# Attention, MoE and soft MoE on one core: w_out turned for its product with phi, converted again after the attention

## The chip, the cores and the metric

The kernel runs on one core of one Trainium2 chip. The metric is the device time of one execution in microseconds (us), the lower the better; times are medians over runs. The engines are TensorE (PE, with its weight loads as PEld), VectorE (DVE), ScalarE (ACT), GpSimd (POOL) and SyncE (SP), which issues every DMA of this kernel.

## What is computed

Three layers, one after the other. Attention with rotary embedding over 4 batches of 8 heads, 576 positions, 64 wide; a feed-forward layer; a soft mixture of 8 experts with 4 slots each. The inputs of the last two, w_in and w_out among them, are float64 arrays; q, k and v are float32.

```python
# attention, then
h = x @ w_in                                   # (2304, 512) @ (512, 2048)
g = np.maximum(h, 0.0) + alpha * np.minimum(h, 0.0)
x = g @ w_out                                  # (2304, 2048) @ (2048, 512)
# soft mixture of experts
logits = x @ phi                               # (2304, 512) @ (512, 32)
d = softmax(logits over tokens); slot_input = d.T @ x
slot_out = relu(slot_input @ w1[e]) @ w2[e]    # 4 slots for each of 8 experts
return softmax(logits over slots) @ slot_out
```

## The kernel before

**The algebra.** x = g @ w_out is never formed. The logits are g @ (w_out @ phi), and the slots' inputs are (d.T @ g) @ w_out. So w_out is wanted twice: early, for the product wph = w_out @ phi (2048 by 32), and late, for the product px = (d.T @ g) @ w_out, after all tokens have been gone through.

**The stages.** The attention runs over 16 pairs of heads (4 batches, 4 pairs each). For a pair PE makes scores (st), DVE takes their maximum (mm), ACT the exponential (e), POOL scales it by the inverse sum (e<-e,mm). The block is then turned: in batch 0 by PE (pt), in batches 1 to 3 by DVE in 32-wide blocks (tb), which go through DRAM (sc) and come back turned (ET). PE then multiplies with v (pv); there are three pv for a pair, 48 in all. Beside the attention, and after it, the feed-forward layer goes over 9 blocks of 256 tokens (the last one gathers the rows beyond 512 of the four batches), each in 16 chunks of 128 hidden columns. A chunk is 12 matmuls (ph), rl on ACT, g on DVE; for two chunks PE turns g (pt) and ACT copies it (gt); for four chunks PE makes the logits (lg) with wph as weights, in four column groups side by side. Each block ends with pu, the sum d.T @ g. After the ninth block come px with w_out, the experts' two layers (ph of L1088, po) and the output (pf).

**The weights before.** prep_w (L593) brings w_in and then w_out in eight pieces each, 1 MB of float64 in a slot "raw", and DVE converts them to float32 by three integer steps (L628, L630, L632). A piece of w_out lands as 256 rows in a buffer of which there is one (wf, the tile w32; the trace calls it w). From there it goes two ways. A DMA stores it to wo_dram, a copy in DRAM in float32 (L659). And wphi (L675), twice for a piece, makes 128 rows of wph: PE turns four 128x128 blocks (wtp, L683), ACT copies them (wt, L687), PE multiplies the four with phi, w_out's blocks as weights and phi's 32 columns moving (wphp, L692), and DVE scales the result into wph (L695). After the attention the copy is read back (wo, L959) into a pool of 26 slots of 512 KB (x), which it shares with the experts' weights (xw, L995).

**What sets the order.** A planner (class Plan) takes every operation with a cost, a due time, what it depends on and the slots that it takes, and writes each engine's instructions in one fixed order. Each engine then runs its own list in order and waits by semaphores where something is not ready. The pool pm has three PSUM buffers, shared by ph, pt, pv, pu, wtp, wphp and others; PE can start a ph only when an earlier one has been read by rl and g.

## Time and profile before

| | |
|---|---|
| median of 3 runs | 688.85 us (685.62 to 688.97) |
| the profiled execution | 688.74 us, of which the span from first to last instruction is 686.9 us |
| mean granted TensorE clock | 0.958 of full speed |
| busy share of the span | PE 92%, PEld 66%, DVE 63%, ACT 48%, POOL 41% |
| moved by DMA | 160.76 MB, mean 234 GB/s |

All times in the rows are counted from the span's start; what lies outside the span, 1.8 us, is the same for any change inside. A busy share over the whole span mixes the stages: about 0 to 140 us (the first batch, with the weights' conversion), to 522 us (batches 1 to 3, with the first blocks of the feed-forward layer beside them), to 618 us (the rest of that layer alone), and the end (px, the experts, the output). So each stage is read by itself: the table of stretches tells how full each engine was, with the granted clock, the share of time in which the DMA engines were busy and what they moved; the timeline shows instructions with the idle time ahead of them in brackets and what ended it; the chain of waits follows the last instruction back through what released each step. Matmuls overlap in PE's pipeline, so a matmul's own duration is longer than its share of PE's time; that is read from one start to the next.

### The profile page before, as it was taken

The numbers are of one execution on the slowest core, as the hardware profiler recorded it, in microseconds if no ns is written. First come the engines' busy times: TensorE is split into PE (matmuls) and PEld (weight loads), VectorE is DVE, ScalarE is ACT, GpSimd is POOL, SyncE is SP. The second block draws the span as 40 slices with busy tenths as digits, with TensorE's granted clock in tenths as the row PEclk, the third lists the DMA queues.
The fourth block names the chain that finished last, engine by engine and source line by source line (L and its number), as shares of the span: only waits on it lengthen the run. The fifth ranks groups of instructions, "written<-read, shape, count | busy, mean of one in ns | idle before, by whom it ended". The sixth has DMA issues, their size and how long they took to land.

```text
span 686.9 us, 13841 instructions
## 1 busy us (share of the span) xinstructions
PE 629.2 (92%) x5168; PEld 453.5 (66%) x5168; DVE 429.7 (63%) x937; ACT 328.7 (48%) x816; POOL 283.4 (41%) x283
## 2 busy tenths in 40 slices
PE   2889979989999999998999999999999999988974
PEld 1555555667978678777777867777686878763442
DVE  5777798776968776686667868575743232334332
ACT  3536446444656566555465655564443433330121
POOL 0797998566237286376365554431210000000000
PEclk9878999968999999999999999999999999999996
DMA  9944275765499999989988989894465950457998
GB/s 302 369 157 148 76 265 177 216 210 181 141 282 253 301 269 290 271 239 267 280 230 253 272 262 269 215 249 137 135 160 211 401 217 9 154 177 274 368 391 284
DMA packets 78306, 160.76 MB, mean 234 GB/s; under 512 B 9888, under 2 KB 39072, under 8 KB 78240
## 3 DMA queue, kind: packets, MB, share of 16 engines
q1 hardware_dynamic: 78240, 159.88, 75.4%
q8 instruction: 41, 0.67, 0.4%
q14 instruction: 25, 0.20, 0.1%
HBM read 104.54 MB, written 34.08 MB: 202 GB/s over the span
## 4 chain that ended last, share of the span: by engine, by line
PE 56%; DMA 23%; DVE 7%; POOL 5%; SPq 4%; issue 2%; ACT 2%; DVEq 0%; ACTq 0%; POOLq 0%
PE ph L720 19%; PE pv L554 10%; DMA ET<-sc 8%; DMA sc<-tb 5%; DMA xw<-in_moe_w_dram 4%; PE st L412 4%; PE st L399 3%; PE pt L739 3%; PE pt L475 2%; PE lg L750 2%; PE pu L844 2%; SPq L508 2%; DMA ks<-xn 2%; PE wphp L692 2%; POOL e L454 2%
## 5 line engine op out<-in xcount | busy, mean ns | idle before, releaser
L454 POOL TENSOR_SCALAR e<-e,mm 128x576 f32<-128x576 f32 x144 | 120.0, 844 | 164.4 <-DVE mm L430 119.5
L720 PE MATMUL ph<-xt,w 128*128 128x256 f16 x1536 | 185.6, 273 | 0.1
L720 PEld LDWEIGHTS <-w 128*128 128x128 f16 x1728 | 163.9, 98 | 31.8 <-issue 11.0
L422 ACT ACTIVATE e<-st,mm 128x576 f32<-128x576 f32 x144 | 106.3, 739 | 43.4 <-DVE mm L417 34.9
L417 DVE TENSOR_REDUCE mm<-st 128x1 f32<-128x576 f32 x144 | 106.1, 744 | 23.3 <-PE st L412 12.6
L733 DVE SCALAR_TENSOR_TENSOR g<-rl,oma,ph 128x256 f32<-128x256 f32 x144 | 68.1, 473 | 82.0 <-ACT rl L728 81.2
L728 ACT ACTIVATE rl<-ph 128x256 f32<-128x256 f32 x144 | 55.2, 383 | 102.1 <-PE ph L720 101.1
L321 POOL TENSOR_TENSOR xn<-xn,tabs 128x576 f32<-128x576 f32 x60 | 88.8, 1491 | 36.7 <-issue 8.2
L554 PE MATMUL pv<-ET,vt 128*64 128x256 f32 x512 | 66.1, 400 | 10.2 <-DMA ET<-sc 8.9
L462 DVE STREAM_TRANSPOSE tb<-e 128x512 f32<-128x512 f32 x96 | 66.6, 700 | 11.9 <-DMA sc<-tb 6.0
L412 PE MATMUL st<-ks,qs 128*128 128x288 f32 x384 | 71.0, 313 | 0.2
L399 PE MATMUL st<-ks 64*128 64x288 f32 (+1 forms) x168 | 46.3, 497 | 16.6 <-DVE ks L329 11.2
L412 PEld LDWEIGHTS st<-ks,qs 128*128 128x128 f32 x384 | 54.5, 191 | 6.1 <-issue 3.3
L554 PEld LDWEIGHTS pv<-ET,vt 128*64 128x64 f32 x512 | 37.3, 141 | 30.8 <-issue 5.0
L744 ACT ACTIVATE gt<-pt 128x512 f32<-128x512 f32 x72 | 43.0, 598 | 12.4 <-PE pt L739 10.2
L399 PEld LDWEIGHTS st<-ks 64*128 64x128 f32 (+1 forms) x168 | 25.8, 209 | 31.1 <-DVE ks L329 11.2
L739 PE MATMUL pt<-idf,g 128*128 128x128 f32 x288 | 43.9, 275 | 0.4 <-DVE g L733 0.4
L564 ACT ACTIVATE xt<-pv,vb 128x256 f16<-128x256 f32 x32 | 15.1, 473 | 53.9 <-PE pv L554 53.9
L324 POOL TENSOR_TENSOR xn<-xn 128x576 f32<-128x576 f32 x24 | 36.0, 1502 | 1.1
L739 PEld LDWEIGHTS pt<-idf,g 128*128 128x128 f32 x288 | 33.4, 141 | 4.2 <-issue 2.4
L475 PE MATMUL pt<-idf,e 128*128 128x128 f32 x192 | 33.7, 310 | 2.6 <-POOL e L454 2.0
L475 PEld LDWEIGHTS pt<-idf,e 128*128 128x128 f32 x192 | 26.0, 163 | 14.2 <-issue 6.1
(155 smaller groups left out, 833.3 us busy)
## 6 DMA issues: line engine op xcount, KB each, us to landing
sc<-tb SPq DMA_DIRECT2D x48, 512.0 KB, 5.8
ET<-sc SPq DMA_DIRECT2D x96, 256.0 KB, 6.0
xw<-in_moe_w_dram SPq DMA_DIRECT2D x42, 512.0 KB, 9.4
ks<-xn SPq DMA_DIRECT2D x96, 144.0 KB, 4.5
xn<-in_k_dram SPq DMA_DIRECT2D x16, 576.0 KB, 5.8
xn<-in_q_dram SPq DMA_DIRECT2D x16, 576.0 KB, 6.6
wraw<-in_moe_w_in_dram SPq DMA_DIRECT2D x8, 1024.0 KB, 7.7
wraw<-in_moe_w_out_dram SPq DMA_DIRECT2D x8, 1024.0 KB, 5.6
```

Of the source, the lines that this page charges most:

```text
L321: eng.tensor_tensor(e["x"][:, w], e["x"][:, w], tabs[:, (0 if z == "q" else 2) + w], ALU.mult)
L399: nc.tensor.matmul(st[to, j, at:at + w], x, k[rows, z:z + w], start=True, stop=True)
L412: nc.tensor.matmul(st[:, j, 0:288], r["q"][:, 768 * h + 128 * s:768 * h + 128 * s + 128].bitcast(F32R), r["k"][:, a, h, ks].bitcast(F32R), ...
L417: nc.vector.tensor_reduce(c["mm"][:, h:h + 1], c["st", h][:, :, 0:288], axis=AX.XY, op=ALU.max, negate=True)
L422: nc.scalar.activation(c["e"][:, h].rearrange("p (a n) -> p a n", a=2), c["st", h][:, :, 0:288], AF.Exp, bias=c["mm"][:, h:h + 1], accum_o ...
L454: nc.gpsimd.tensor_scalar(c["e"][:, h], c["e"][:, h], c["mm"][:, 6 + h:7 + h], 1.0, ALU.mult, ALU.mult)
L462: nc.vector.transpose(out=c["tb"][:, :, h].rearrange("p (q m) j -> p q m j", q=4), in_=c["e"][:, h, 64 * h:64 * h + 512].rearrange("p (m q ...
L475: nc.tensor.transpose(c["pt", h][:, i], c["e"][:, h, 64 * h + 128 * i:64 * h + 128 * i + 128], idf)
L554: nc.tensor.matmul(pv[r], v[k, 4 * h + i if i < 4 else 8], x, start=(i == 0), stop=(i == 4))
L720: nc.tensor.matmul(ph, wi[j][:, wp, kc, 128 * fo:128 * fo + 128], xt[:, xp, kc, :], start=(n == 0), stop=(n == 3 * KC - 1),)
L733: nc.vector.scalar_tensor_tensor(blk["g", j][:, fo, :], c["r"], oma[:, f:f + 1], c["ph"], ALU.mult, ALU.add)
L739: nc.tensor.transpose(c["pt"][:, t, i, :], blk["g", j][:, fo - 1 + i, 128 * t:128 * t + 128], idf)
```

## The change

The host hands the kernel w_out a second time, turned (w_out_t, 512 by 2048). The early path loads pieces of w_out_t instead of w_out, 256 of its columns at a time, and converts them as before. The product with phi now has phi as weights: each of the four 128-row parts of phi is loaded into its own group of 32 columns (tile_position), all four multiply side by side into one PSUM tile (wpp), each giving a partial sum over its part of w_out's columns. ACT copies that (wt), and two matmuls with the columns' selector sel4 as moving operand turn it and add up the four groups (wphp). One wphi serves 256 rows of wph, so there are 8 in place of 16. The store to wo_dram is gone. When the attention ends, sixteen pieces of w_out in its natural form, 512 KB of float64 each, are loaded into slots of the pool x, and DVE converts each of them by the same three integer steps into the eight wo tiles, from which px reads as before. These loads are due ahead of the experts' weights.

```diff
-            if which == 0:
-                src = w_in[:, PF * j:PF * j + PF].rearrange("(c p) f -> p c f", p=128)
-            else:
-                src = w_out[PF * j:PF * j + PF, :].rearrange("(c p) f -> p c f", p=128)
-            nc.sync.dma_start(raw[:].rearrange("p (c f) t -> p c (f t)", c=src.shape[1]), src.bitcast(I32))
+            src = (w_in, w_out_t)[which][:, PF * j:PF * j + PF].rearrange("(c p) f -> p c f", p=128)
+            nc.sync.dma_start(raw[:].rearrange("p (c f) t -> p c (f t)", c=KC), src.bitcast(I32))
...
-            wo_saved.append(op(DMA, 1500, due, lambda: nc.sync.dma_start(wo_dram[:, 2 * j:2 * j + 2, :], c["wo"]), [o], uses=[s_w]))
-            for i in range(2):
-                wphi(2 * j + i, i, c, o, s_w, due + WS)
+            wphi(j, c, o, s_w, due + WS)
...
-        def turn():
-            c["p"] = ps_m.tile([128, KC, 128], F32, tag="pm", name="wtp")
+        def parts():
+            c["p"] = ps_m.tile([128, PF], F32, tag="pm", name="wpp")
             for i in range(KC):
-                nc.tensor.transpose(c["p"][:, i, :], w["wo"][:, z, 128 * i:128 * i + 128], idf)
+                nc.tensor.matmul(c["p"][32 * i:32 * i + 32, :], phs[:, i, :], w["wo"][:, i, :], start=True, stop=True, tile_position=(0, 32 * i))
...
         def mults():
-            c["q"] = ps_m.tile([128, NS], F32, tag="pm", name="wphp")
-            for i in range(KC):
-                nc.tensor.matmul(c["q"], c["t"][:, i, :], phs[:, i, :], start=(i == 0), stop=(i == KC - 1))
+            c["q"] = ps_m.tile([128, 2, NS], F32, tag="pm", name="wphp")
+            for z in range(2):
+                nc.tensor.matmul(c["q"][:, z], c["t"][:, 128 * z:128 * z + 128], sel4[:, 0], start=True, stop=True)
...
-        def reload(j=j):
-            wo[j] = xp["p"].tile([128, 2, 512], F32, tag="x", name="wo")
-            nc.sync.dma_start(wo[j], wo_dram[:, 2 * j:2 * j + 2, :])
-
-        wo_op[j] = op(DMA, 1456, 1000 + WO_AT, reload, [att_done] + wo_saved, takes=[s_wo[j]], uses=[s_wo[j]])
+        def load():
+            c["raw"] = xp["p"].tile([128, 512, 2], I32, tag="x", name="wor")
+            nc.sync.dma_start(c["raw"], w_out[128 * f:128 * f + 128, :].bitcast(I32).rearrange("p (d t) -> p d t", t=2))
+
+        def conv(step):
+            lo, hi = c["raw"][:, :, 0], c["raw"][:, :, 1]
+            if step == 0 and not z:
+                wo[j] = xp["p"].tile([128, 2, 512], F32, tag="x", name="wo")
+            x = wo[j][:, z].bitcast(I32)
+            if step == 0:
+                nc.vector.tensor_scalar(x, hi, 3, 0x3FFFFFFF, ALU.logical_shift_left, ALU.bitwise_and)
+            elif step == 1:
+                nc.vector.scalar_tensor_tensor(x, lo, 29, x, ALU.logical_shift_right, ALU.bitwise_or)
+            else:
+                nc.vector.scalar_tensor_tensor(x, hi, -0x40000000, x, ALU.bitwise_and, ALU.bitwise_or)
+
+        d = 990 + 0.1 * f
+        o = order_ops["wo"] = op(DMA, 1456, d, load, [att_done, order_ops.get("wo")], takes=[s_raw], uses=[s_raw])
+        o = op(DVE, 450, d, lambda: conv(0), [o, wo_op.get(j)], takes=[] if z else [s_wo[j]], uses=u)
+        o = op(DVE, 750, d, lambda: conv(1), [o], uses=u)
+        wo_op[j] = op(DVE, 700, d, lambda: conv(2), [o], uses=u)
```

The planner then orders all engines anew. Three places show it. On PE, in batch 0 (st are scores, pt and pc turn the exponentials e, pv multiplies with v, w32 is a converted piece of w_out), the kernel before has:

```order
L683 MATMUL wtp_1048<-idf_94,w32_988 128x128 x4
L399 MATMUL st_1054<-ks_705 128x288 x2
L692 MATMUL wphp_1070<-phs_104,wt_1058 128x32 x4
L475 MATMUL pt_1079<-idf_94,e_986 128x128 x4
L683 MATMUL wtp_1090<-idf_94,w32_988 128x128 x4
L475 MATMUL pt_1098<-idf_94,e_986 128x128 x4
L399 MATMUL st_1105<-ks_705 128x288 x2
L518 MATMUL pc_1109<-idf_94,e_986 128x128
L399 MATMUL st_1114<-ks_705 128x288 x2
L692 MATMUL wphp_1119<-phs_104,wt_1103 128x32 x4
L475 MATMUL pt_1131<-idf_94,e_1065 128x128 x4
```

and with the change:

```order
L676 MATMUL wpp_1060<-w32_984,phs_104 32x256 x4
L475 MATMUL pt_1066<-idf_94,e_961 128x128 x4
L518 MATMUL pc_1080<-idf_94,e_961 128x128
L685 MATMUL wphp_1084<-sel4_106,wt_1076 128x32 x2
L399 MATMUL st_1089<-ks_704 128x288 x2
L475 MATMUL pt_1097<-idf_94,e_1015 128x128 x4
L554 MATMUL pv_1103<-ET_986,vt_150 64x256 x8
L554 MATMUL pv_1103<-ec_1024,vt_150 64x256 x2
```

A piece of w_out took two sets of wtp and wphp, 16 matmuls, and takes one wpp and one wphp, 6 matmuls; the scores, turns and pv around it stay, in a somewhat other order. The last of the 8 wpp stands ahead of the first ph, where before four of the 16 sets stood among the ph.

On DVE, behind the end of the attention (dn, sacc, ssum and lp belong to a block's end, g to its chunks), the kernel before has:

```order
L836 TENSOR_SCALAR dn_6357<-pd_6339,vb_107 128x64
L733 SCALAR_TENSOR_TENSOR g_6327<-rl_6370,oma_113,ph_6344 128x256
L853 SCALAR_TENSOR_TENSOR sacc_117<-sacc_117,sts_115,pu_6361 128x512
L859 SCALAR_TENSOR_TENSOR ssum_114<-ssum_114,sts_115 128x1
L733 SCALAR_TENSOR_TENSOR g_6327<-rl_6397,oma_113,ph_6375 128x256
L733 SCALAR_TENSOR_TENSOR g_6434<-rl_6430,oma_113,ph_6399 128x256
L733 SCALAR_TENSOR_TENSOR g_6434<-rl_6441,oma_113,ph_6417 128x256
```

and with the change, in a stretch of chunks of that stage:

```order
L967 TENSOR_SCALAR wo_6399<-wor_6282 128x512
L969 SCALAR_TENSOR_TENSOR wo_6301<-wor_6256,wo_6301 128x512
L728 SCALAR_TENSOR_TENSOR g_6404<-rl_6401,oma_112,ph_6368 128x256
L971 SCALAR_TENSOR_TENSOR wo_6301<-wor_6256,wo_6301 128x512
L728 SCALAR_TENSOR_TENSOR g_6404<-rl_6413,oma_112,ph_6386 128x256
L969 SCALAR_TENSOR_TENSOR wo_6399<-wor_6282,wo_6399 128x512
L967 TENSOR_SCALAR wo_6451<-wor_6322 128x512
L971 SCALAR_TENSOR_TENSOR wo_6399<-wor_6282,wo_6399 128x512
L728 SCALAR_TENSOR_TENSOR g_6404<-rl_6453,oma_112,ph_6421 128x256
L967 TENSOR_SCALAR wo_6399<-wor_6303 128x512
L728 SCALAR_TENSOR_TENSOR g_6404<-rl_6464,oma_112,ph_6438 128x256
```

Between two g, which followed each other directly, now stand one to five steps of the conversion (wor is a piece of w_out as loaded, wo the converted tile).

On SP, the queue of DMA issues, at the end of the attention (sc and ET are its shuttle through DRAM), the kernel before has:

```order
L508 DMA ET<-sc 32x8x256 x4
L995 DMA xw<-in_moe_w_dram 128x1024 x18
L959 DMA wo<-wo_dram 128x1024 x2
L995 DMA xw<-in_moe_w_dram 128x1024
L959 DMA wo<-wo_dram 128x1024 x6
L995 DMA xw<-in_moe_w_dram 128x1024
L995 DMA xw<-in_moe_w_dram 128x2x1024 x7
```

and with the change:

```order
L499 DMA sc<-tb 128x1024 x2
L508 DMA ET<-sc 32x8x256 x4
L959 DMA wor<-in_moe_w_out_dram 128x1024 x16
L1014 DMA xw<-in_moe_w_dram 128x1024 x20
L1014 DMA xw<-in_moe_w_dram 128x2x1024 x7
```

The sixteen loads of w_out stand ahead of the experts' weights, where the eight reloads stood behind eighteen of them.

## Rows read from the trace of the kernel before

**Rows 1.** Stretches: us, busy us (instructions) of PE, PEld, DVE, ACT, POOL; clock, DMA share, GB/s
```profile
90.00:140.00 50.00, 44.79 (x283) 29.65 (x283) 41.71 (x68) 27.74 (x65) 37.83 (x33) 0.93 0.70 225
140.00:195.00 55.00, 53.52 (x387) 43.34 (x386) 43.84 (x87) 27.76 (x70) 27.65 (x27) 0.84 0.60 181
195.00:250.00 55.00, 52.03 (x465) 40.16 (x464) 39.94 (x89) 31.71 (x86) 28.66 (x30) 1.00 0.99 282
...
540.00:580.00 40.00, 39.91 (x372) 31.39 (x371) 13.07 (x30) 15.56 (x36) 0.00 (x0) 1.00 0.48 186
```

**Rows 2.** Chain of waits, 85 to 200 us: shares by line; pieces with start and us
```profile
by line: PE pv L554 13.1%; PE st L399 11.9%; PE wphp L692 10.7%; PE pt L475 6.5%; DMA ET<-sc 5.3%; PE ph L720 4.7%; PE wtp L683 4.3%; SPq L352 4.1%; issue 3.9%; DVE wx L630 3.8%; PE st L412 3.8%; DVE wx L632 3.0%; POOL e L454 2.9%; DVE xn L
...
143.06 0.61 ACT wt L687
...
166.27 1.08 PE wphp L692 x8
...
198.45 1.70 PE pv L554 x13
```

**Rows 3.** Groups by form: count, busy us, mean ns, then idle us before and releaser
```profile
L750 PE MATMUL lg<-g,wph 128*32 128x256 f32 x288 | 23.0, 391 | 0.0
...
L692 PE MATMUL wphp<-phs,wt 128*128 128x32 f32 x128 | 18.4, 290 | 2.2 <-ACT wt L687 2.2
```

**Rows 4.** Timeline of PE around two sets of lg: start, us, instruction, idle before
```profile
187.41 0.64 PE L750 MATMUL lg<-g,wph 128*32 128x256 f32 x8
187.98 1.08 PE L692 MATMUL wphp<-phs,wt 128*128 128x32 f32 x8
...
548.89 2.52 PEld L720 LDWEIGHTS <-w 128*128 128x128 f16 x24 [0.41 <-issue]
548.90 2.79 PE L720 MATMUL ph<-xt,w 128*128 128x256 f16 x24
```

**Rows 5.** Chain of waits, the pu that end two successive blocks
```profile
561.54 1.85 PE pu L844 x16
...
591.98 1.85 PE pu L844 x16
```

**Rows 6.** Timeline of DVE, conversion of the first piece of w_in, POOL idle
```profile
14.24 0.68 DVE L628 TENSOR_SCALAR w<-wraw 128x1024 int32<-128x1024 int32 x1
...
15.51 1.22 DVE L630 SCALAR_TENSOR_TENSOR w<-wraw,w 128x1024 int32<-128x1024 int32 x1
```

**Rows 7.** Timeline of DVE and PE after the attention, two pairs of chunks
```profile
550.84 0.48 DVE L733 SCALAR_TENSOR_TENSOR g<-rl,oma,ph 128x256 f32<-128x256 f32 x1 [1.94 <-ACT rl L728]
...
551.96 2.78 PE L720 MATMUL ph<-xt,w 128*128 128x256 f16 x24
...
552.14 0.48 DVE L733 SCALAR_TENSOR_TENSOR g<-rl,oma,ph 128x256 f32<-128x256 f32 x1 [0.83 <-ACT rl L728]
...
553.89 0.48 DVE L733 SCALAR_TENSOR_TENSOR g<-rl,oma,ph 128x256 f32<-128x256 f32 x1 [1.27 <-ACT rl L728]
```

**Rows 8.** DMA issues, us to landing: 521:523, 526:530 (xw), whole span (wraw)
```profile
xw<-in_moe_w_dram SPq DMA_DIRECT2D x3, 512.0 KB, 5.4
...
xw<-in_moe_w_dram SPq DMA_DIRECT2D x5, 512.0 KB, 9.6
...
wraw<-in_moe_w_in_dram SPq DMA_DIRECT2D x8, 1024.0 KB, 7.7
wraw<-in_moe_w_out_dram SPq DMA_DIRECT2D x8, 1024.0 KB, 5.6
```

**Rows 9.** The page: moved by DMA in 40 equal slices of 17.2 us
```profile
GB/s 302 369 157 148 76 265 177 216 210 181 141 282 253 301 269 290 271 239 267 280 230 253 272 262 269 215 249 137 135 160 211 401 217 9 154 177 274 368 391 284
```

**Rows 10.** Stretches of 1 us, PE alone: busy us, granted clock, DMA share, GB/s
```profile
143.00:144.00 1.00, 0.29 (x3) 1.00 1.03 360
144.00:145.00 1.00, 1.00 (x8) 0.50 0.48 105
...
161.00:162.00 1.00, 1.00 (x9) 0.96 1.05 400
```

More of the change, by code (lines that the diff above doesn't have):

```diff
@@ L162, in attn_moe_softmoe @@
 @with_exitstack
-def attn_moe_softmoe(ctx, tc, qx, kx, vx, w_in, w_out, alpha, phi, w1, w2, tab, msks, out):
+def attn_moe_softmoe(ctx, tc, qx, kx, vx, w_in, w_out, alpha, phi, w1, w2, tab, msks, w_out_t, out):
     nc = tc.nc
@@ L581, in attn_moe_softmoe @@
     wi = {}
-    wo_dram = dram.tile([128, FC, DM], F32, name="wo_dram")
-    wo_saved = []
     w_ops = {}
@@ L601, in load @@
             raw = c["raw"] = wgt.tile([128, 1024, 2], I32, tag="w", name="wraw")
[L602 to L608 removed]
+            src = (w_in, w_out_t)[which][:, PF * j:PF * j + PF].rearrange("(c p) f -> p c f", p=128)
+            nc.sync.dma_start(raw[:].rearrange("p (c f) t -> p c (f t)", c=KC), src.bitcast(I32))
+        a_, f_ = ((2, 128), (1, 256))[which]
         def conv(step):
@@ L953, in attn_moe_softmoe, with late_w @@
     wo, s_wo, wo_op = {}, {}, {}
-    for j in range(NPC):
-        s_wo[j] = Slot("x")
-        def reload(j=j):
-            wo[j] = xp["p"].tile([128, 2, 512], F32, tag="x", name="wo")
-            nc.sync.dma_start(wo[j], wo_dram[:, 2 * j:2 * j + 2, :])
-        wo_op[j] = op(DMA, 1456, 1000 + WO_AT, reload, [att_done] + wo_saved, takes=[s_wo[j]], uses=[s_wo[j]])
+    def late_w(f):
+        c, j, z = {}, f // 2, f % 2
+        s_raw = Slot("x")
+        if not z:
+            s_wo[j] = Slot("x")
+        u = [s_raw, s_wo[j]]
+        def load():
[17 more added lines that the diff above has]
+        wo_op[j] = op(DVE, 700, d, lambda: conv(2), [o], uses=u)
+    for f in range(FC):
+        late_w(f)
     NX = NB - 4
@@ L1355 @@
     form = {"q": _keys, "k": _keys, "v": _values, "moe2_w2": _second}
-    data = [(name, form[name](_np, a) if name in form else a) for name, a in data] + _tables(_np)
+    turned = [("w_out_t", _np.ascontiguousarray(a.T)) for name, a in data if name == "moe_w_out"]
+    data = [(name, form[name](_np, a) if name in form else a) for name, a in data] + _tables(_np) + turned
     for name, a in data:
```

21 lines of the change are left out of this document (11 added, 10 removed).

## The prediction

> **What bounds the kernel now.** The first view is the table of stretches. From 140 us to the end of the attention TensorE (PE) is busy for all but some percent of the time, and from 540 to 580 us for 39.91 of 40 us [rows 1]; POOL and ACT are far from full there. In 195 to 250 us the DMA share is 0.99 as well, so the attention of batches 1 to 3 is bound by two things at once, PE and the shuttle of transposed blocks through DRAM; after the attention the DMA falls idle while PE stays full. The second view is the chain of waits from 85 to 200 us, the stretch of the work that the change replaces. Before about 108 us it runs through DVE and POOL, from there to 185 us almost only through PE: of its 115 us, 10.7% are wphp, 4.3% wtp [rows 2]. So a PE microsecond taken out there is worth up to one microsecond, unless DMA, DVE or the clock takes it back.
>
> **What goes.** On the chain stand 12.3 us of wphp and 4.9 us of wtp (the two shares of 115 us), and three waits of PE for the copy wt on ACT, about 0.7 us each (the copy's 0.61 us, and the hand-overs; PE's own idle time ahead of wphp is 2.2 us in all) [rows 2, 3]. That is 17.2 + 2.1 = 19.3 us. The rest of the 16 sets lies beside DVE and POOL work and counts for nothing.
>
> **What comes in its place.** Eight times four wpp matmuls, 32 columns of weights by 256 moving, f32, in four column groups. That is the shape of lg, whose eight records take 187.41 to 187.98 us, 0.57 us, until the next starts [rows 4]. Then two matmuls with the shape of wphp, half of a set of four, 0.5 us (sets at full clock take 1.08 us with their overlap) [rows 2]. 8 x 1.07 = 8.6 us, all put on the path. Bounds: 6.5 of the 8 on the path give 7 us; four groups one after another instead of side by side would be eight records of 0.39 us [rows 3], 3.1 us a set, 25 us in all and 29 with the second step. I take 8.6, since the row has the same shape and the same four groups. So PE is relieved of 10.7 us.
>
> A rule speaks against this: the Trainium skill, TensorEngine Tiling (Array Packing), Key Properties, says that changing the tiling mode drains TensorE. The trace agrees in so far as the weight load behind an lg stands idle for 0.41 us, at 548.89 us, with PE's matmul 0.01 us behind it [rows 4]; but the 0.57 us run from start to next start, so a drain is in them. Were 0.41 us a switch to come on top at 16 switches, 6.6 us of the relief would be gone, and the sum at the end would be 689.0.
>
> **Where the relief lands.** The order shows it. Ahead of the 13th pv (198.45 us before [rows 2]) PE had 8 ph chunks done and now has 12; ahead of the 48th and last, 96 before and 98 now. A chunk costs 1.9 us of PE: 16 of them and their dispatch take 591.98 - 561.54 = 30.4 us [rows 5]. So of 10.7 us, 7.6 go into four chunks done early, and 3.1 us make the 13th pv earlier. From there to the end of the attention two chunks fewer are left: 3.8 us if PE is the bound, nothing if the DMA is (0.99 [rows 1]); between the two I take the middle, 1.9. After the attention two chunks fewer remain, on a PE without gaps: 3.8 us. Sum 3.1 + 1.9 + 3.8 = 8.8 us.
>
> **The late conversion.** Sixteen times three DVE steps on 128x512, behind the attention's end. On 128x1024 with POOL idle a tensor_scalar took 0.68, a scalar_tensor_tensor 1.22 us [rows 6]; halved, 0.34 + 0.61 + 0.61 = 1.6 us each, 25 us in all. The order spreads the 48 steps over 23 chunks, about 44 us, in which DVE has 23 x 0.48 = 11 us of g; it ends up some 85% full. What hides them: the gaps ahead of g, 0.83 and 1.27 us by turns (longer when lg stands between) [rows 7]. The order puts one step in the short gaps, two or three in the long ones, so a g is late by 0.1 to 0.4 us. What that may cost: the next ph but one needs g's PSUM buffer; g at 550.84 us ends at 551.32 and that ph starts at 551.96, so some 0.6 us are spare [rows 7]. Most lateness vanishes there. The first step waits for its load: the first loads of this stretch land 5.4 us after issue, later ones 9.6 [rows 8], and behind that waiting step stand g and the sacc update, for which PE waits through its three PSUM buffers. Conversions then come every 2.75 us, loads every 1.3 us (512 KB at about 400 GB/s [rows 9]), so only the first can be late. I take 2.5 us; bounds 0 and, if every step were uncovered, 25 us.
>
> **Edits taken at nothing.** Eight stores to wo_dram and eight reloads go; nothing on PE waits for them. SP now issues 16 raw loads of 512 KB first, then the expert weights, which wait for conversions to free slots. That is 4.2 MB more; covered by the DMA's idle time from 567 to 618 us (9, 154, 177 GB/s where 391 are possible: 17.2 us x 833 = 14 MB [rows 9]); without this cover 4.2 MB would cost 10.7 us. The weights for ph at 630 us then have 50 us to spare, and the tail (weights in slots that wo frees) keeps its order. The turned w_out comes in 2 KB runs, as w_in does: 7.7 against 5.6 us to land [rows 8]; three raw slots hide it. ACT loses 16 copies of 0.6 us and gains 8 shorter ones; DVE loses eight small scalings. The wf buffer no longer waits for a store, so the eight conversions of w_out move earlier, into a stretch with DVE 83% busy [rows 1]; that is why the 13th pv is only 3.1 us earlier in my sum.
>
> **Sum.** 688.74 (profiled execution; the median of the runs shown is 688.85) - 8.8 + 2.5 = 682.4 us.
>
> **Rivals.** (1) All of the relief is won and more. PE ran at half clock from 144 to 161 us, after idle time at 143 us [rows 10]; the waits for wt are part of that idling (143.06 us, [rows 2]). Without them the stretch may stay at 2.4 GHz: 17.4 us at half speed, less the 5.5 us of wphp and wtp in it already counted, halved: 6 us. 688.74 - 10.7 - 6 + 2.5 = 674.5. Against it: less work leaves more gaps, not fewer.
> (2) DMA and DVE bind: the 13th pv comes no earlier, the shuttle takes as long; left are the 3.8 us behind the attention, 688.74 - 3.8 + 2.5 = 687.4. For it: DMA 0.99; against it: PE's few idle microseconds.
> (3) The late conversion surfaces: DVE's fixed order makes g late beyond its 0.6 us. At 0.3 us lost for each of 48 steps, 14.4 us: 694.3, slower. It decides from 8.8 / 48 = 0.18 us a step. For it: DVE 85% full; against: the order fits steps to gaps.
> (4) A second stretch at half clock: with PE thinner from 90 to 165 us, another 17.4 us at 1.2 GHz where PE is the bound costs 8.7: 688.74 - 8.8 + 2.5 + 8.7 = 691.1. The Trainium skill, TensorE: Matmul & The Clock Gate, Part 1, says that the clock is 1.2 GHz after idling and 2.4 after sustained work; the trace agrees with the fall behind the idle 143rd us. By that rule alone, thinning PE's work would give this fourth time.
> (5) The column groups run one after another: 29 instead of 8.6 us, 702.
>
> **Chances.** Forecast 0.47 (own range 679 to 685.5), rivals 0.16, 0.18, 0.10, 0.07, 0.02. The range 672 to 690 takes in (1) and (2) and most of the forecast, and leaves out (3), (5) and half of (4). A measurement tells about 0.5%, 3.4 us, from no change: faster 0.61 (forecast but for its edge, and 1), same 0.22 (2, the edge, a little of 4), slower 0.17.
>
> **What will show it.** Right: wpp sets of about 0.57 us; 12 ph chunks ahead of the 13th pv, and that pv near 195 us; the last pv near 517 us; PE still without gaps from there to the last pu; conversions done some 45 us after the attention; the tail from px on as long as now. Wrong: clock below 1.00 in other stretches than before, ph waiting for DVE's g after the attention, the 13th pv at 198 us or later, expert weights waited for at ph (L1107), or wpp records that do not overlap.

## The result, and the profile with the change

| | before | with the change |
|---|---|---|
| median | 687.09 us (682.01 to 690.38, 20 runs) | 694.91 us (688.71 to 698.22, 20 runs) |
| ratio, 95% interval | | 1.0121 [1.0096, 1.0145] |
| profiled execution, its span | 688.74 us, 686.9 us | 689.75 us, 687.6 us |

The change makes the kernel slower by 1.2%, some 8 us, where 6.3 us of gain were forecast. The profiled execution of before is one of its slower ones, that of the change one of its faster ones; so the two traces differ by less than the medians, and where a few us matter the runs below decide, not these two traces. Ratios leave disturbed runs out, so they can stand a little off the ratio of two medians.

The work itself shrank as expected. First the page's busy line, then groups by form (count, busy us, mean ns, idle us before and releaser), then the timeline of PE around a set of wpp, all of the changed kernel:

```profile
PE 609.0 (89%) x5072; PEld 435.0 (63%) x5072; DVE 454.0 (66%) x977; ACT 323.5 (47%) x808; POOL 289.6 (42%) x283
```

```profile
L971 DVE SCALAR_TENSOR_TENSOR wo<-wor,wo 128x512 int32<-128x512 int32 x16 | 10.9, 685 | 0.1
L969 DVE SCALAR_TENSOR_TENSOR wo<-wor,wo 128x512 int32<-128x512 int32 x16 | 10.8, 685 | 0.0
...
L967 DVE TENSOR_SCALAR wo<-wor 128x512 int32<-128x512 int32 x16 | 6.3, 422 | 1.2 <-DMA wor<-in_moe_w_out_dram 1.2
...
L676 PE MATMUL wpp<-w,phs 128*32 128x256 f32 x64 | 6.0, 452 | 0.1
...
L685 PE MATMUL wphp<-sel,wt 128*128 128x32 f32 x32 | 5.3, 290 | 1.4 <-ACT wt L680 1.1 <-ACT ec L522 0.4
```

```profile
105.84 0.64 PE L676 MATMUL wpp<-w,phs 128*32 128x256 f32 x8
106.41 1.25 PE L399 MATMUL st<-ks 64*128 64x288 f32 x8
```

A set of wpp goes from 105.84 to 106.41 us, 0.57 us, exactly the price taken from lg [rows 4]. wpp and wphp together are busy for 11.3 us, where wphp alone was busy for 18.4 [rows 3]. PE is at 89% of the span where it had 92%. But the time that PE no longer needs has become waiting. The stretches (as in rows 1: busy us of PE, PEld, DVE, ACT, POOL; clock, DMA share, GB/s):

```profile
90.00:140.00 50.00, 39.16 (x257) 22.77 (x255) 43.96 (x68) 23.11 (x56) 41.80 (x31) 0.87 0.65 200
140.00:195.00 55.00, 51.27 (x387) 38.49 (x387) 40.84 (x84) 29.82 (x79) 28.28 (x28) 0.87 0.48 126
195.00:250.00 55.00, 51.38 (x460) 40.55 (x460) 38.20 (x86) 30.10 (x79) 29.10 (x30) 1.00 0.91 254
250.00:300.00 50.00, 43.78 (x375) 32.76 (x375) 34.56 (x79) 25.96 (x69) 24.80 (x26) 0.97 0.94 261
...
350.00:400.00 50.00, 44.56 (x389) 33.40 (x388) 34.19 (x80) 26.98 (x69) 28.24 (x30) 1.00 0.97 266
...
540.00:580.00 40.00, 39.19 (x368) 31.19 (x366) 31.51 (x66) 15.29 (x35) 0.00 (x0) 1.00 0.87 331
```

From 90 to 140 us PE is busy for 39.16 us, where it was for 44.79 [rows 1], while POOL rose from 37.83 to 41.80 and DVE to 43.96 of 50. From 250 to 300 us and from 350 to 400 us PE stands idle for 5 to 6 us in 50, with the DMA at 0.94 to 0.97; before, it stood idle for about 1 us in each:

```profile
250.00:300.00 50.00, 48.65 (x439) 38.28 (x436) 35.94 (x82) 30.92 (x81) 30.68 (x29) 1.00 0.97 267
...
350.00:400.00 50.00, 49.30 (x444) 37.45 (x441) 37.39 (x83) 30.48 (x78) 27.14 (x29) 1.00 0.90 253
```

From 540 to 580 us, where the late conversion lies, PE is almost as full as before. The chain of waits from 85 to 200 us says the same, for the same stretch as rows 2:

```profile
by line: POOL e L454 8.5%; PE ph L715 7.0%; DMA sc<-tb 6.7%; DMA ET<-sc 6.4%; PE st L399 6.0%; DVE mm L417 5.9%; PE pv L554 5.8%; PE pt L475 4.4%; DMA qs<-xn 4.2%; DVE w L627 3.9%; POOL xn L321 3.5%; DMA xn<-in_k_dram 3.5%; DVE mm L429 3.2%
```

wphp, 10.7% of it before, is gone from its head; POOL and the shuttle (sc, ET) stand there now.

### The profile page after: what moved, and what is told of

Its sections match the earlier page's. It is cut to its first block, busy times and chain, and to the rows that moved or that the text cites. A ratio compares the mean times of both kernels' runs of the same rounds, so it can differ in the third digit from the quotient of the medians.

```text
span 687.6 us, 13685 instructions
## 1 busy us (share of the span) xinstructions
PE 609.0 (89%) x5072; PEld 435.0 (63%) x5072; DVE 454.0 (66%) x977; ACT 323.5 (47%) x808; POOL 289.6 (42%) x283
## 4 chain that ended last, share of the span: by engine, by line
PE 53%; DMA 19%; DVE 11%; POOL 7%; SPq 3%; ACT 2%; issue 2%; DVEq 0%; POOLq 0%; ACTq 0%
PE ph L715 20%; PE pv L554 9%; DMA ET<-sc 5%; DMA sc<-tb 5%; PE st L412 4%; DMA xw<-in_moe_w_dram 4%; PE pt L734 3%; POOL e L454 3%; PE st L399 3%; DVE mm L417 2%; PE lg L745 2%; DMA xn<-in_k_dram 2%; PE pu L839 2%; PE pt L475 2%; SPq L508 2%
## 5 line engine op out<-in xcount | busy, mean ns | idle before, releaser
L454 POOL TENSOR_SCALAR e<-e,mm 128x576 f32<-128x576 f32 x144 | 121.9, 857 | 164.9 <-DVE mm L430 113.8
L321 POOL TENSOR_TENSOR xn<-xn,tabs 128x576 f32<-128x576 f32 x60 | 91.5, 1539 | 37.3 <-DMA ET<-sc 12.3
L399 PE MATMUL st<-ks 64*128 64x288 f32 (+1 forms) x168 | 44.6, 497 | 16.9 <-DVE ks L329 11.3
L564 ACT ACTIVATE xt<-pv,vb 128x256 f16<-128x256 f32 x32 | 15.2, 474 | 64.6 <-PE pv L554 64.6
L399 PEld LDWEIGHTS st<-ks 64*128 64x128 f32 (+1 forms) x168 | 25.6, 213 | 30.4 <-DVE ks L329 11.3
L475 PE MATMUL pt<-idf,e 128*128 128x128 f32 x192 | 32.2, 300 | 4.7 <-POOL e L454 4.7
L567 DVE SCALAR_TENSOR_TENSOR xt<-pv,vb,xt 128x256 f16<-128x256 f32 x32 | 15.4, 480 | 30.7 <-ACT xt L564 30.7
```

The costliest lines, as they stand in the source:

```text
L321: eng.tensor_tensor(e["x"][:, w], e["x"][:, w], tabs[:, (0 if z == "q" else 2) + w], ALU.mult)
L399: nc.tensor.matmul(st[to, j, at:at + w], x, k[rows, z:z + w], start=True, stop=True)
L454: nc.gpsimd.tensor_scalar(c["e"][:, h], c["e"][:, h], c["mm"][:, 6 + h:7 + h], 1.0, ALU.mult, ALU.mult)
```

## The experiments

Three times place a loss. The 13th pv is the first of the second batch, the 48th ends the attention; each is dated by ACT taking it over (xt, L564). The fifth column is the time from the 48th pv to the last pu. The last one counts, in PE's order, the ph chunks ahead of the 13th and of the 48th pv; with 1.9 us a chunk [rows 5] it tells how much of a shift is only work done sooner or later. All times are from single profiled executions, which lie up to 6.5 us under their kernel's median (e_42; the changed kernel 5.2), so a few us in a column mean nothing. With before's early work and order, or nearly, the 13th pv is dated 195.9 to 201.5 (f_before34, b_late, before).

| kernel | ratio to before | 13th pv | 13th to 48th | 48th to last pu | chunks ahead of 13th, 48th |
|---|---|---|---|---|---|
| before | 1 | 201.5 | 320.7 | 100.0 | 8, 96 |
| changed | 1.0121 | 199.0 | 327.2 | 95.9 | 12, 98 |
| changed, again | 1.0108 [1.0069, 1.0147] | 201.0 | 326.7 | 96.0 | 12, 98 |
| c_early | 1.0120 [1.0070, 1.0170] | 204.9 | 324.6 | 95.9 | 12, 98 |
| d_early_old | 0.9977 [0.9941, 1.0013] | 193.3 | 320.8 | 100.0 | 8, 96 |
| d2_full_old | 1.0027 [0.9991, 1.0064] | 197.5 | 322.2 | 101.2 | 8, 96 |
| b_late | 1.0013 [0.9984, 1.0041] | 198.5 | 317.3 | 103.6 | 8, 96 |
| e_28 | 0.9931 [0.9899, 0.9962] | 189.8 | 325.7 | 95.9 | 10, 98 |
| e_spread | 0.9906 [0.9870, 0.9942] | 188.4 | 323.3 | 100.4 | 10, 96 |
| e_42 | 0.9965 [0.9924, 1.0005] | 176.3 | 341.8 | 95.3 | 8, 98 |
| c_early34 | 0.9939 [0.9912, 0.9965] | 189.1 | 323.1 | 99.5 | 10, 96 |
| f_before34 | 1.0017 [0.9987, 1.0047] | 195.9 | 322.6 | 99.9 | 9, 96 |
| g_cheap | 1.0200 [1.0158, 1.0242] | 213.1 | 316.7 | 103.0 | 14, 94 |
| g_cheap34 | 1.0334 [1.0298, 1.0369] | 209.5 | 327.0 | 100.2 | 11, 96 |

The kernel before had medians of 684.1 to 685.2 us beside these runs, so 0.01 in a ratio is 6.8 us.

### Early part, late part, order

after_again is the changed kernel once more. c_early is its early part and order, without the late conversion: plain loads of w1 stand in place of w_out's natural form, so px is not the reference's.

```diff
-            nc.sync.dma_start(c["raw"], w_out[128 * f:128 * f + 128, :].bitcast(I32).rearrange("p (d t) -> p d t", t=2))
-  (three DVE steps for each of 16 pieces)
+            nc.sync.dma_start(wo[j], w1[j, 0:128, :].rearrange("p (a f) -> p a f", a=2))
```

d_early_old issues c_early's instructions, but in the order of the kernel before: the planner is given the old sixteen sets with their old costs, and the second set of a piece issues nothing. d2_full_old is the whole change in that old order.

```diff
-            wphi(j, c, o, s_w, due + WS)
+            wo_saved.append(op(DMA, 1500, due, lambda: None, [o], uses=[s_w]))
+            for i in range(2):
+                wphi(2 * j + i, i, c, o, s_w, due + WS)
...
-        o = op(PE, 550, due - ATT, parts, [dep, phs_op], takes=[s_p], uses=[s_p, s_w])
+        o = op(PE, 430, due - ATT, nothing if z else parts, [dep], takes=[s_p, s_t], uses=[s_p, s_t, s_w])
```

> The changed kernel once more, for a second trace and as the measure for the others on the same chip. Every theory expects about 695 us beside about 687 us for the kernel before. Theory A (the planner's new order of the attention is worse than the old one, whatever work it orders) and theory C (thinner work on TensorE makes it run more often at 1.2 GHz) differ in the trace: by A the clock's share stays near 0.96 and the time between the 13th and the 48th pv is longer than the 320 us of before; by C the mean clock is below 0.955 and the loss lies where the clock is at 0.50.

> The early part of the change alone, in the changed kernel's order: the late conversion is left out, eight plain loads of 512 KB of other data take its place, so the output is not that of the reference. Theory A (order of the attention): still slow, 691 to 694 us, the late conversion being worth 1 to 3 us. Theory B (the late conversion on DVE and its loads cost the time): 684 to 688 us, as fast as before or faster. Theory C (clock): 691 to 695 us.

> The same instructions as in the run c_early, but in the order of the kernel before: the planner is told the old operations with their old costs and each second one of them issues nothing. The late conversion is left out as there. Theory A (order): 680 to 687 us, no slower than before, since PE is relieved by 11 us and nothing else moved. Theory B (late conversion): the same 684 to 688 us as c_early. Theory C (clock, thinner work on TensorE): slow in this order too, 691 to 695 us.

> The whole change, late conversion included, in the order of the kernel before up to the end of the attention. Theory A (order): 682 to 689 us, d_early_old and 1 to 3 us for the conversion. Theory B (late conversion): 692 to 697 us, as slow as the changed kernel. Theory C (clock): 692 to 697 us, with a mean clock below 0.955.

c_early is as slow as the whole change, so the late conversion is not the cause. The same instructions in the old order are at 0.9977: the order alone costs 0.0143, 9.8 us. The stretches of c_early, then of d_early_old:

```profile
90.00:140.00 50.00, 40.36 (x248) 23.38 (x249) 40.97 (x64) 22.59 (x56) 38.82 (x30) 0.83 0.66 206
...
250.00:300.00 50.00, 44.16 (x396) 34.56 (x395) 36.58 (x83) 28.56 (x76) 22.11 (x24) 1.00 1.00 273
...
350.00:400.00 50.00, 45.84 (x399) 34.90 (x398) 34.30 (x80) 27.99 (x73) 28.02 (x28) 1.00 0.98 265
```

```profile
90.00:140.00 50.00, 41.59 (x259) 24.33 (x259) 42.63 (x71) 27.44 (x67) 41.78 (x36) 0.93 0.68 215
...
250.00:300.00 50.00, 47.74 (x416) 36.15 (x414) 36.24 (x84) 28.42 (x75) 29.12 (x29) 1.00 0.98 270
...
350.00:400.00 50.00, 47.74 (x433) 36.84 (x431) 37.74 (x86) 29.98 (x79) 24.15 (x28) 1.00 1.00 268
```

In the new order PE does 1.2 to 3.6 us less in each of these stretches of 50, and 284.8 us for 295.8 from 195 to 500 us. From 250 to 400 us the DMA engines are as busy in both (0.89 to 1.00), so there is little slack in which a worse order could hide. The 13th pv is 11.6 us later in c_early, of which the four more chunks ahead of it are 7.6; the stretch from there to the 48th has two chunks fewer and still takes 3.8 us more. And d_early_old itself shows that shorter work on PE is worth little in an unchanged order: 1.6 us (from a gain of 4.0 to a loss of 0.9), where the forecast had 8.8.

b_late is the counterpart: the early work and order of before, without the copy to DRAM, with the new late conversion.

> The kernel before with its early work and its order, without the copy of w_out to DRAM, and with the changed kernel's late part: w_out's natural form is loaded after the attention and turned into its two halves by DVE. The late part alone: if it is hidden, as PE's 39.2 busy us of 40 between 540 and 580 us say, 683 to 686 where the kernel before has 684; if it costs what the whole change in the old order has over the early part alone in the old order (4.2 us), 686 to 690. Against the whole change in the old order (1.0027 of before) it tells what PE's shorter early work is worth there: the same ratio if nothing, 1.006 or more if some 3 us.

1.0013: the late part costs 0.9 us (from a gain of 1.1 to a loss of 2.8). The whole change in the old order, 1.0027, is no better than this, so there too the shorter early work brought nothing that can be measured.

### A wait at the head of SP's queue

In the new order SP waits longer for the slots of two transfers, of v (L290) and of q and k (L352), with the shuttle's stores and reads queued behind it. Waits of SP's queue from 195 to 530 us (total us, times, longest), first the changed kernel, then d_early_old:

```profile
SPq L290 <- PE pv L554: 27.0, 5, 6.2
...
SPq L352 <- PE st L410: 14.3, 6, 6.6
```

```profile
SPq L290 <- PE pv L554: 9.4, 3, 4.6
...
SPq L352 <- PE st L410: 6.3, 4, 2.7
```

A sixth v buffer takes the wait at L290 away. To make room, v_vt6 keeps small row statistics in tiles that exist already. v_slim has that without the sixth buffer.

```diff
-                e["t"] = att.tile([128, 9, D], F32, tag="vt", name="vt", bufs=5)
+                e["t"] = att.tile([128, 9, D], F32, tag="vt", name="vt", bufs=6)
...
-    rinv = cst.tile([128, 18], F32, name="rinv")
-    lm = cst.tile([128, 18], F32, name="lm")
+    lms = [sw[:, 0:6], mws[:, 18:24], al[:, 0:6]]
+    rinv = mws
```

> The changed kernel with a sixth buffer for the v tiles (five before), fitted in by keeping the router's small row statistics in tiles that are already there; the order of the work on every engine is that of the changed kernel. Theory Q (the new order puts v loads at the head of SP's in-order queue before a v buffer is free, so that stores and reads of the shuttle behind them wait): the waits of SP on pv at L290 between 195 and 530 us fall from 25 to 27 us to under 10, the stretch from the 13th pv to the last falls from about 327 us to 321 to 323, and the time from 692 to 686 to 689 where the kernel before has 684. Theory B (the time is lost on the engines, in the first 200 us and by how the chunks are laid between the heads, and SP's wait is only their echo): SP's wait falls or moves to the next load, and the time stays within 2 us of the changed kernel, 690 to 694.

> The changed kernel with the router's small row statistics kept in tiles that are already there, as v_vt6 has them, but with the five v buffers of the changed kernel: the control of v_vt6, which took 700.1 us. If the slimming costs nothing: 690 to 694, and the 8 us that v_vt6 lost are those of v loads that leave earlier. If v_vt6's loss is of the slimming: 698 to 702.

v_slim: 1.0178 [1.0129, 1.0228], v_vt6: 1.0207 [1.0159, 1.0255]. The wait at L290 left SP's list and nothing was won; these are v_vt6's waits:

```profile
SPq L352 <- PE st L410: 38.1, 6, 9.7
SPq L508 <- DMA sc<-tb: 37.6, 14, 6.7
```

The next ones in the queue grew from 17.1 and 27.5 us in v_slim (14.3 and 23.7 in the changed kernel), so that the three waits together stay as long: 75.7 us for 73.3. The wait at L290 by itself costs nothing that can be measured (1.0207 beside 1.0178); whether SP's queue as a whole does is not shown by this. Why v_slim is some 4 us slower than the changed kernel, with every engine's order the same up to the router, is taken up below.

### How close together the pieces of w_out stand

The planner puts the sixteen pieces (8 of w_in, 8 of w_out) 2.2 apart in its due times. With a shorter chain behind each, and no store holding the one wf buffer, it then draws the conversions of w_out together. The last step of a conversion (L632 before, L627 with the change), for w_out's eight pieces: count, shortest, median and longest ns, first and last start, in before, in the changed kernel, in e_spread, e_28 and g_cheap (the last two kernels come below):

```profile
L632 DVE SCALAR_TENSOR_TENSOR w<-wraw,w x8: 1175/1218/1718, 88.2 to 184.3; 128x1024 int32<-128x1024 int32 x8
```

```profile
L627 DVE SCALAR_TENSOR_TENSOR w<-wraw,w x8: 1204/1410/1755, 85.0 to 155.6; 128x1024 int32<-128x1024 int32 x8
```

```profile
L627 DVE SCALAR_TENSOR_TENSOR w<-wraw,w x8: 1204/1434/2135, 86.8 to 175.2; 128x1024 int32<-128x1024 int32 x8
```

```profile
L627 DVE SCALAR_TENSOR_TENSOR w<-wraw,w x8: 1212/1436/1815, 86.8 to 160.7; 128x1024 int32<-128x1024 int32 x8
```

```profile
L632 DVE SCALAR_TENSOR_TENSOR w<-wraw,w x8: 1210/1377/1821, 89.1 to 182.0; 128x1024 int32<-128x1024 int32 x8
```

From the first to the last that is 96 us before, 71 in the changed kernel, 88 in e_spread, 74 in e_28 and 93 in g_cheap.

e_spread is the changed kernel with one number more, 3.4 for w_out's pieces; e_28 and e_42 have 2.8 and 4.2 there. f_before34 is the kernel before with the same line, c_early34 is c_early with it. (w_out has eight such pieces; where an expectation says sixteen, these are meant.)

```diff
-            prep_w(j, which, W0 + W1 * (j + NPC * which))
+            prep_w(j, which, W0 + W1 * NPC * which + (3.4 if which else W1) * j)
```

> The changed kernel with the due times of the sixteen pieces of w_out 3.4 apart in place of 2.2, so that their conversions on DVE and GpSimd are spread over the heads as they stood in the kernel before; the planner lays the rest around them. Theory B (the early conversions stand too close together in the new order, at score steps 17 to 34 in place of 17 to 43, and fill DVE and GpSimd between 90 and 140 us): score steps 24 to 30 take 18 to 22 us in place of 27, the 13th pv ends near 194 to 197 us in place of 199 to 205, and the time is 684 to 689 where the kernel before has 684. Theory Q (SP's queue in batches 1 to 3 is what costs): the 13th pv may come earlier, but the stretch from it to the last pv stays at 325 to 328 us, and the time is 689 to 694.

> The changed kernel with the pieces of w_out due 2.8 apart: between the changed kernel (2.2, ratio 1.012) and e_spread (3.4, ratio 0.9906). Theory B (a dose: the more the conversions are spread, the sooner the 13th pv): ratio between the two, 0.995 to 1.008, 13th pv 190 to 198 us. Theory L (the planner's order is a throw of dice by 1 to 2% for any change of its numbers, and the spread is not what counts): the ratio lies outside 0.99 to 1.012, or the 13th pv shows no order by the spacing.

> The changed kernel with the pieces of w_out due 4.2 apart, more than e_spread's 3.4. Theory B: the 13th pv as early as in e_spread or earlier, 184 to 190 us, and a ratio of 0.985 to 0.995, unless the last piece now ends so late that the chunks start late, which shows as more chunks left after the last pv (over 101 us from it to the last pu in place of 100.4). Theory L: a ratio over 1.0 with a 13th pv later than 192 us though the conversions are spread wider.

> The kernel before, whole and with its own costs, with the one number of e_spread: the due times of the sixteen pieces of w_out 3.4 apart in place of 2.2. It tells whether e_spread's 0.9906 is the changed work's gain once its order is spread, or the gain of the spread alone. Theory B1 (the kernel before is spread already by its own longer chain, at score steps 17 to 43, and the gain of e_spread is the shorter early work): 683 to 689 where the kernel before has 684 to 685. Theory B2 (spreading helps any kernel of this family by the same 1%): 676 to 680, and the change itself is worth nothing.

> The changed kernel's early part with the pieces of w_out due 3.4 apart, in e_spread's order, but without the late conversion: the natural form of w_out is not computed, plain loads of w1 stand in its place, so that the output is not the reference's. e_spread (the same with the late conversion) is 0.9906 of before. If the late conversion is hidden behind PE after the attention: 0.988 to 0.9925. If it costs the 4.2 us that the whole change in the old order has over its early part: 0.982 to 0.986, about 674 where the kernel before has 685.

One number in the order takes the changed kernel from 1.2% slower to 0.9% faster: 0.0215, 14.7 us, with not an instruction added or removed; that is some 5 us more than either theory expected of it. Its stretches:

```profile
90.00:140.00 50.00, 42.84 (x260) 25.86 (x259) 45.75 (x70) 26.22 (x63) 42.07 (x32) 0.85 0.63 194
140.00:195.00 55.00, 53.30 (x457) 40.13 (x456) 46.44 (x95) 31.85 (x83) 30.94 (x30) 0.95 0.67 185
...
250.00:300.00 50.00, 46.36 (x400) 35.50 (x399) 37.79 (x87) 27.93 (x75) 28.85 (x30) 0.97 0.94 252
```

From 90 to 195 us PE, DVE and ACT all get more done than in the changed kernel (PE 96.1 for 90.4 us, DVE 92.2 for 84.8, ACT 58.1 for 52.9), and PE issues 717 matmuls for 644. The three copies of the 13th pv, in the changed kernel, in e_28 and in e_spread:

```profile
198.57 0.47 ACT L564 ACTIVATE xt<-pv,vb 128x256 f16<-128x256 f32 x1 [3.27 <-PE pv L554]
```

```profile
189.28 0.47 ACT L564 ACTIVATE xt<-pv,vb 128x256 f16<-128x256 f32 x1 [1.97 <-PE pv L554]
```

```profile
187.92 0.47 ACT L564 ACTIVATE xt<-pv,vb 128x256 f16<-128x256 f32 x1 [0.99 <-PE pv L554]
```

In these traces the 13th pv comes earlier as the spacing grows: 199.0, 189.8, 188.4 and, at 4.2, 176.3 us. Two, two and four chunks fewer stand ahead of it, which is 3.8, 3.8 and 7.6 us of that, and the 1.4 us between e_28 and e_spread are within the traces' scatter. e_42 then takes 341.8 us for the rest of the attention, with 90 chunks in it where the changed kernel has 86: 7.6 of its 14.6 us more are the chunks put off, the rest stays open. e_42's twelve runs go from 679.93 to 692.64 us, and their median, 687.64, is over before's 684.61; its ratio of 0.9965 is no gain. e_28 won somewhat more than was expected of it, e_42 less.

The number steers the order; that it does so through the distance between the conversions is not shown. e_28's stand as close as c_early's (74 us from first to last in both), and e_28 is at 0.9931 where c_early is at 1.0120. Nor does the spacing mend the place where the change loses: counted at 1.9 us a chunk, and against the kernels in the old order (317.3 to 322.2 us for 88 chunks), the stretch from the 13th to the 48th pv is dearer by an estimated 8 to 11 us in the changed kernel and c_early, and by 5 to 7 still in e_28, e_spread and c_early34. What these three win, they win ahead of the 13th pv.

The spread alone does nothing for the kernel before (1.0017). The old work was not run in e_spread's own order, so how much of e_spread's 0.9% is the change's and how much a better order's is not known. And c_early34, 0.9939 [0.9912, 0.9965], beside e_spread's 0.9906 finds the late conversion free in this order as well, though it is itself a little slower than was expected.

### Is it the bunching, in any kernel?

g_cheap is the kernel before with all its work, and with the planner's costs of the turn and the products lowered to half of the new ones, since the old work has two sets for a piece (PE 430 to 275 and 1100 to 225, ACT 600 to 180, DVE 100 to 65). The planner also no longer counts the wf buffer as held by the store, which at run time it still is. g_cheap34 adds the spacing of 3.4.

```diff
-            wo_saved.append(op(DMA, 1500, due, lambda: nc.sync.dma_start(wo_dram[:, 2 * j:2 * j + 2, :], c["wo"]), [o], uses=[s_w]))
+            wo_saved.append(op(DMA, 1500, due, lambda: nc.sync.dma_start(wo_dram[:, 2 * j:2 * j + 2, :], c["wo"]), [o]))
...
-        o = op(PE, 1100, due - ATT, mults, [o, phs_op], takes=[s_q], uses=[s_t, s_q])
+        o = op(PE, 225, due - ATT, mults, [o, phs_op], takes=[s_q], uses=[s_t, s_q])
```

> The kernel before with all its work (turns, phi products, the copy of w_out through DRAM), but with the planner's costs of the turn, its copy and the products lowered to those of the changed kernel, so that only the order differs. Theory O (any new order that the planner lays from cheaper early work costs, whatever the work is): 690 to 697 where the kernel before has 684. Theory W (it is this change's own work that costs in its new place): 682 to 688, within 0.6% of the kernel before.

> The kernel before with all its work and the planner's lowered costs (g_cheap, ratio 1.020), and the pieces of w_out due 3.4 apart in place of 2.2. Theory B (lowered costs draw the conversions together, and that is what costs, whatever the early work is): ratio 0.995 to 1.006, 13th pv 196 to 203 us in place of 213. Theory L (the lowered costs move other things too, the planner's order is a throw): 1.012 to 1.025, and the 13th pv stays over 207 us.

Another order makes the old work slower too, by 2.0%. But spacing does not bring it back; it makes it worse, 3.3%, over what either theory expected. And g_cheap's conversions were never drawn together: they take 93 us from first to last, where before's take 96. So it is shown that the order costs, and that in the changed kernel the due times of w_out's pieces steer it. That bunched conversions are the bad thing in an order is not shown; g_cheap, and e_28 beside c_early, speak against it. These two kernels are also ordered by costs that do not fit their work: from 60 to 215 us DVE waits 9.3 and 12.4 us for products (wphp) that the planner took for cheaper, where before it waits 3.6; for the store of wf it waits at most 2.9 us. So their 2.0 and 3.3% need not have the cause of the changed kernel's 1.2%. What makes an order of this planner good stays open.

### Where the tiles lie

v_slim leaves out two tiles of 72 bytes a partition, and everything allocated behind them moves: the weight pool, the attention's tiles, the tiles of the experts. All the kernels of the table in The experiments have these at the same addresses, as read from the built programs; the traces hold no addresses. a_pad is the changed kernel with an unused tile, b_pad the kernel before with the same one, v_pad is v_slim with two unused tiles in the old place, e_384 is e_spread moved by 384 bytes.

```diff
+    pad = cst.tile([128, 36], F32, name="pad")
```

> The changed kernel with an unused tile of 144 bytes a partition beside the router's row statistics: the same instructions in the same order on every engine, and the tiles that lie behind it 144 bytes further on. If where the tiles lie doesn't count: 690 to 694 (ratio 1.008 to 1.016). If v_slim's 7 us (the two tiles of 72 bytes taken out, order kept) are of the place: a ratio outside that, 0.99 to 1.005 or 1.02 and more.

> v_slim with two unused tiles of 72 bytes where the row statistics lay, so that all tiles lie again where the changed kernel has them; the statistics stay in the borrowed tiles. If v_slim's 7 us come from the place of the tiles: 690 to 694 (1.008 to 1.016). If they come from the borrowed tiles (waits that the sharing brings): 697 to 702 (1.016 to 1.023).

> The kernel before, same instructions and same order, with an unused tile beside the row statistics that moves the weight and attention tiles 160 bytes further on. In the changed kernel the same move took the time from 1.0115 to 1.0274 of before, and the DMA engines moved 265 GB per busy second in place of 273 to 277 between 195 and 500 us. Theory P (misplaced tiles make every DMA transfer of the attention slower, in any order): 1.010 to 1.020, and 262 to 268 GB per busy second. Theory I (it is the changed kernel's order that the slower transfers hit, the kernel before has room): 0.997 to 1.006 with the same slower transfers.

> e_spread (pieces of w_out due 3.4 apart) with an unused tile that moves the weight and attention tiles 384 bytes further on, a multiple of 128, so that they start at a multiple of 512 bytes (before: 128 over one). Theory P with steps of 128 bytes: as e_spread, 0.987 to 0.994 of before. If a multiple of 512 is better still: under 0.986, and over 280 GB per busy second between 195 and 500 us. If any move costs: 1.000 or more.

| kernel | moved by | start of these tiles, modulo 256 bytes | ratio |
|---|---|---|---|
| changed, v_pad | 0 | 128 | 1.0121, 1.0115 [1.0072, 1.0159] |
| v_slim | -192 bytes | 192 | 1.0178 [1.0129, 1.0228] |
| a_pad | 160 bytes | 32 | 1.0274 [1.0243, 1.0304] |
| before | 0 | 128 | 1 |
| b_pad | 160 bytes | 32 | 1.0115 [1.0077, 1.0152] |
| e_spread | 0 | 128 | 0.9906 [0.9870, 0.9942] |
| e_384 | 384 bytes | 0 | 0.9872 [0.9826, 0.9918] |

The stretch from 195 to 500 us, in before, b_pad, the changed kernel, a_pad, e_spread and e_384:

```profile
195.00:500.00 305.00, 294.22 (x2612) 226.44 (x2611) 215.36 (x483) 173.84 (x457) 148.41 (x157) 0.99 0.90 248
```

```profile
195.00:500.00 305.00, 288.70 (x2576) 222.61 (x2577) 212.79 (x475) 170.05 (x446) 147.02 (x155) 1.00 0.92 244
```

```profile
195.00:500.00 305.00, 284.55 (x2528) 220.61 (x2529) 211.13 (x472) 168.98 (x441) 146.11 (x155) 0.99 0.89 244
```

```profile
195.00:500.00 305.00, 277.83 (x2431) 213.98 (x2430) 200.44 (x458) 163.84 (x429) 144.80 (x153) 0.98 0.91 241
```

```profile
195.00:500.00 305.00, 291.27 (x2560) 222.56 (x2559) 213.99 (x475) 170.32 (x447) 149.01 (x158) 0.99 0.87 242
```

```profile
195.00:500.00 305.00, 292.72 (x2599) 225.31 (x2598) 214.49 (x479) 172.53 (x453) 149.11 (x158) 0.99 0.86 244
```

The last two columns divided give GB/s while the DMA engines are busy: 276 before and 265 in b_pad; 274 changed and 265 in a_pad; 278 in e_spread and 284 in e_384. The move by 160 bytes makes every busy DMA microsecond worth 3 to 4% less, and the kernel pays 1.2 to 1.5% for it in either order. The engines' own work does not get slower by it: over the span DVE is busy for 429.7 us before and 429.6 in b_pad, ACT for 328.7 and 328.6, POOL for 283.4 and 284.0. And the loss lies between the 13th and the 48th pv, where the shuttle runs: 326.0 us in b_pad for 320.7, 337.3 in a_pad and 333.8 in v_slim for 327.2; from the 48th pv to the last pu none of them differs by more than 0.5 us. So the DMA is a bound of that stretch, which the forecast had seen and met by taking the middle, 1.9 us, between 3.8 and nothing. The place has no part in the verdict on the change, since before and changed kernel agree in it. It accounts for v_slim: with the place restored, v_pad is back at 1.0115 and at 246 / 0.88 = 280 GB/s while busy, though the intervals of the two ratios overlap.

The fastest kernel found is e_384, 676.47 us (674.36 to 680.31), 1.3% under the kernel before; from e_spread (678.50 us) the intervals do not part it.

## Why the prediction was wrong, point by point

**The work's price: right.** wpp took 0.57 us a set; the late steps 0.42 and 0.69 us where 0.34 and 0.61 were taken; the late conversion's cost between a gain of 2.3 us (e_spread beside c_early34) and a loss of 3.4 (d2_full_old beside d_early_old), where +2.5 was taken; the stretch after the attention shorter by 4.1 us for two chunks, where 3.8 was.

**Where the relief lands: the step that failed.** Of its three terms (3.1, 1.9 and 3.8 us) the last stands. The second has the other sign: from the 13th to the 48th pv the two traces of the changed kernel take 6.5 and 6.0 us more, not 1.9 less, with two chunks fewer in it. Of the first the two traces have 2.5 and 0.5 us, and c_early, in the same order, has the 13th pv 3.4 us later; nothing clear of the traces' scatter. The sum was read from PE's share of the chain, 10.7% wphp: but much of what was taken from PE there went into waiting for DVE, POOL and the shuttle, which the chain of the changed kernel has at its head. The chain of before ran from 108 to 185 us through PE for 65.6 of 77 us, somewhat less than "almost only". A share of the chain is the most that can be won, and d_early_old measured what could, in the old order: 1.6 us in place of 8.8.

**The new order at nothing: the same step's other half.** The prediction counted chunks ahead of each pv in the order, and took the order to run as well as the old one. It did say that the conversions of w_out move into a stretch with DVE 83% busy, and put no price on that. The order costs 9.8 us (c_early beside d_early_old), against a relief of 1.6 us and a late part that costs nothing in this order (after_again beside c_early: 0.8 us of gain). 9.8 - 1.6 - 0.8 = 7.4 us is after_again's 1.0108; the three differences run through the same kernels, so that they add up is no further proof. Why this order costs is not shown.

**The rivals.** Rival 2 (DMA and DVE bind) was nearest in mechanism: the relief of PE wins next to nothing in the old order, and moving the tiles shows the DMA as a bound. It lacked the order's price, and it forecast 1.3 us of gain where d_early_old with the late part (d2_full_old) is at 1.0027; that 687.4 and d2_full_old's 687.19 us agree is chance, since before took 688.74 us in the one and 684.19 in the other. Rival 3 (late conversion) falls: c_early. Rival 4 (a second stretch at half clock) falls for the most part: the granted clock from 90 to 195 us is 0.87 in the changed kernel and, over the same 105 us, 0.89 before, worth some 2 us. Over whole runs the mean clock is 0.960 in after_again and 0.965 in before beside it; among the runs of either kernel 0.005 of clock goes with about 2 us, so by this estimate no more than 2 of the 7 us hang on it. Rival 1: no clock was won. Rival 5: the groups overlap (its sum is 702.8, not 702).

**By accident right in size.** e_spread gains 6.4 us, about the forecast's sum. It does not save the forecast: its 13th pv is 13 us earlier than in the trace of before and its attention then 2.6 us longer, none of which is the forecast's reckoning.

## What to carry to other kernels

Where a planner or scheduler orders the work, a change of costs is a change of order, and the order must be priced: run the new work in the old order and the old work in the new order before judging the work. In this kernel PE and the DMA were both nearly full, and PE time taken away was at most won and mostly turned into waiting; one due time was worth nearly twice what the change itself cost, and how a better order is found stays open. A shift of a pv or of a stretch is read with the chunks counted that lie ahead of it. When a tile is added or left out, compare tile addresses too.

## What the runs showed of the hardware

That 160 bytes of place in SBUF cost 8 to 11 us, with every instruction and its order unchanged, was not expected. Tiles that start at a multiple of 256 bytes (most of them of 512 too; the runs do not tell the two apart) were served at 284 GB/s of busy DMA time, at 128 over it with 274 to 280, at 32 over it with 265; v_slim, at 192 over it, had 243 / 0.92 = 264.

The Trainium skill, DMA: Bandwidth & Descriptors, How a descriptor splits into AXI transactions, says that a descriptor that does not start at a multiple of 256 bytes fetches from the boundary below, so that bytes are moved for nothing. The one run at a multiple of 256 agrees by its GB/s, 284 beside e_spread's 278, though its time is not clear of e_spread's. By that rule, as an estimate, a start at 32 would waste less than one at 128; here it was the slower one, 265 beside 276 GB/s, and the measurement decides.

The four column groups of wpp ran side by side with 0.57 us from the set's start to the next instruction's, with a 128x128 matmul directly ahead and a 64-row one behind: no drain beyond that was seen.
